# Two products in one vector instruction: the scan's steps and the power tables of a gated attention and state-space kernel

## The chip, the cores and the metric

The kernel runs on one core of a Trainium2 chip. The metric is the device time of one execution in microseconds; the median of three runs is given. The engines are called PE (TensorE, matrix products), ACT (ScalarE, here almost only exponentials), DVE (VectorE), POOL (GpSimd) and SP (the engine that issues most transfers).

## What is computed

Two branches over the same 2048 positions of 512 channels, mixed by a gate per position. Cut to what matters:

```python
g = sigmoid((x * gate_w).sum(-1, keepdims=True))
# a: attention with 32 heads of 16
p = softmax(q @ k.T * 16 ** -0.5)            # per head, 2048 x 2048
a = (p @ v, heads joined) @ wo
# b: a state-space layer, 512 channels with 128 complex states
logdA = exp(log_dt) * (A_re + 1j * A_im)
K[d, l] = real(sum_n C[d, n] * exp(logdA[d, n] * l) * exp(log_dt) * B[d, n])
b = causal_convolution(x, K) + x * Dskip
out = g * a + (1 - g) * b
```

## The kernel before

**Attention.** The 32 heads times 2048 queries times 2048 keys are cut into 2048 tiles of 128 keys by 512 queries. Four tiles (four heads at the same keys) are a *quad*, 64 tiles a *block*; there are 32 blocks. Tiles are taken in 683 groups of three: PE writes the scores of a group into one of two PSUM tiles `SC` (`qk`), ACT takes the exponential of the whole group in one activation (`ex`, line 907) into the ring `ET`, and PE multiplies by the values (`pv`) into `OA`. Transposes and normalizing of a finished block (`norm_a`, `norm_b`, `norm_c`) are on DVE.

**Exponentials on DVE.** Some tiles are done by DVE instead. A *set* is one quad of keys whose four tiles are taken out of four consecutive groups, one from each (`SHAPE`), so that the activation has two tiles in place of three. DVE turns the scores into the bits of an approximate power of two (`bits`, line 943, into `DZ`), and two further instructions per set (`batch`, line 954) make two shifted copies (`DU`, then `DZ` again); PE sums the three with values scaled for them (`VS`, made in `vscaled`, line 929). Sets are only allowed in windows of the group number (`WIN`: from group, to group, how many sets may be in flight, how many classes of key tiles), for which buffers have to fit into SBUF.

**State-space branch.** The convolution is done in chunks of 64 positions. `params` computes powers of the complex factor per channel and state on DVE: `L1`, `L2`, ... `L48`, and `MU`, the factor of a whole chunk; the copies `D16`, `D32`, `D48` (line 1145) hold each value twice side by side, as bf16. `base` makes the first 16 powers (`B16`), and `table` the other 48 from them: for each of eight pairs of channel blocks, for each m in 1 to 3 and for the real and the imaginary part, two products of 1024 columns into `tt1` and `tt2`, and their difference or sum into `PT` (all recorded by the helper `tt`, line 1001). That is 48 parts. `kstage` makes the convolution's kernel within a chunk from the tables, `sstage` the sums that each chunk hands on (evicted at line 1304 into `SG`; 16 blocks, marks `S0` to `S15`), and `scan` runs over the chunks. It has two halves of 256 channels (`scan0`, `scan1`), each 30 steps on DVE:

| line | what a step does, 512 columns of fp32 each |
|---|---|
| 1331 | `s2` = G (real, imaginary) times the real part of MU |
| 1333 | `s3` = G (imaginary, real) times the imaginary part of MU, negated for the first |
| 1336 | `s2` = `s2` + SG of this chunk |
| 1339 | `G` = `s2` + `s3` |
| 1342 | SG of this chunk = `G`, as bf16 |

The state `G` makes the steps a chain. `ystage` then turns the states into outputs (loads `yloads`, `xyloads`; products from `Py` and `Tt`; line 1415).

**What sets the order.** The program is written by a planner at build time. It keeps a clock per engine with a cost for every instruction, and picks at each point the piece of work (a generator's next step) that could start first; priorities break ties, and work that is not ready within 0.02 us is ranked as if it started 0.3 us from now at the earliest. The groups of attention are the backbone: after each activation, `fill` adds other work until the clock of ACT has been reached; work on PE may run `OVER` past it. `FILL` is a floor of PE work, counted in columns over the last `HWIN` = 3 us; what is missing is filled with products of zeros (`zero`). `DLAG` is the delay the planner assumes from a DVE result to PE, `DMARG` the one after a transfer, `PTM` that after the store of a table. A new set is begun in `decide` when a window and a buffer are open and DVE has collected enough idle time in the planner's clock:

```python
            plan["used"] = max(plan["used"], idle() - DVCAP)
            if plan["set"] is None and clear(x) and idle() - plan["used"] >= dvq():
                plan["used"] += dvq()
```

`dvq()` takes the first entry of `DVQ` whose mark has been passed. So the number of sets, and with it the work of ACT, follows from the idle time that the planner sees on DVE.

Dependences on the same engine count as well: a DVE instruction that reads what an earlier one wrote waits on DVE's own semaphore for it.

Of the kernel before, what the change touches and what calls it, by code (L numbers as in the profile page):

```python
# [13 lines left out]
P = 128  # L14
# [8 lines left out]
HALF_PI = math.pi / 2  # L23
NDSEM = 56
ZCOL = .216 / 512
FILL = 3500
EVERY = 2
XAT = "base0"
HWIN = 3.0
OVER = .6  # L30
DLAG = 0.6
TURN = dict(F=.105, R=.105, C=.105, H=.06)
DMARG = 2.4
PTM = 5.0
ZLAG = .6
BARE = 1
NS = 15
# [8 lines left out]
LEFT = 4  # L46
VSW = 152
VSP = [len(k) * VSW for k in VKT]  # L48
VSAT = (158, 500)
WIN = ((170, 475, 2, 1), (475, 540, 3, 1), (540, 678, 4, 2))  # L50
DVQ = (("scan1", 0.0), ("scan0", 0.5), ("S15", 1.0), (None, 0.5))
BP = 2.2
DVCAP = 2.0
BUP = 1
VW = 136
VG = 4 * VW + 16

# [355 lines left out]
def declare(nc, es):  # L413
    B = {}

    def sb(name, free, dt=BF16):
        B[name] = Buf(name, "sb", free, dt)


    sb("KT", 4 * S)  # L420
    sb("Q", 512)
    sb("Qs", 4 * 512)
    sb("Qm", 2 * 512)
    sb("VE", 16 * VG)
# [48 lines left out]
    for n in ("L1", "L2", "L4", "L8", "L16", "L32", "L48"):  # L473
        sb(n, 2 * D, FP32)
    sb("MU", 3 * D, FP32)
    sb("pt1", 2 * D, FP32)
    sb("pt2", 2 * D, FP32)
    for n in (16, 32, 48):
        for k in range(4):
            sb(f"D{n}.{k}", 4 * P)  # L480

    sb("FP", 2 * 128 * 8, FP32)
    sb("ft1", 2 * 64 * 8, FP32)
    sb("ft2", 2 * 64 * 8, FP32)
    for k in range(4):
        sb(f"B16{k}", 2 * 128 * 16)

    sb("PT", 2 * 2 * CB * T)
    sb("tt1", 2 * CB * 16)
    sb("tt2", 2 * CB * 16)  # L490
    sb("Qt", 2 * 32 * 128)
    sb("Kst", 2 * 8 * P)

    sb("SG0", 33 * 2 * SGH)
    sb("SG1", 33 * 2 * SGH)
    sb("G", 2 * 256, FP32)
    for n in ("s2", "s3"):
        sb(n, 2 * 256, FP32)
# [111 lines left out]
def record(nc, p, B, ins):  # L610
# [458 lines left out]
    def params():  # L1069
# [69 lines left out]
        for o, x, y in (("L16", "L8", "L8"), ("L32", "L16", "L16"), ("L48", "L16", "L32"), ("MU", "L32", "L32")):  # L1139
            yield from cmul("DVE", o, x, y)  # L1140
            if o != "MU":
                for k in range(4):
                    yield ("DVE", .35)
                    d, l = B[f"D{o[1:]}.{k}"], B[o]
                    op("DVE", lambda v, d=d, l=l, k=k: v.tensor_copy(d(0, [[2 * P, 2], [2, P], [1, 2]]), l(P * k, [[D, 2], [1, P], [0, 2]])),
                       [(l, 0)], [(d, 0)], c=.34)
# [15 lines left out]
        sch.mark("wb")  # L1162
        MU = B["MU"]
        yield ("DVE", 0.4)
        op("DVE", lambda v: v.tensor_scalar(MU(2 * D, [[1, D]]), MU(D, [[1, D]]), -1.0, None, ALU.mult), key("MU"), [(MU, 1)], c=.4)
        sch.mark("scanpar")

    def base(qr, eng):
# [36 lines left out]

    def table():
        yield ("AFTER", "D48")
        t1, t2 = B["tt1"], B["tt2"]
        H10 = dv(1024, 2)
        for pb in range(NBLK // 2):  # L1210
            qr, blks = pb // 2, (2 * pb, 2 * pb + 1)
            yield ("AFTER", f"base{qr}")
# [11 lines left out]
            for m in range(1, 4):  # L1224
                Dm = B[f"D{16 * m}.{qr}"]
                for part in range(2):
                    for ti, xr, yr in ((t1, 0, part), (t2, 1, 1 - part)):
                        yield ("DVE", H10)
                        tt("DVE", lambda ti=ti: ti(0, [[16, 2 * CB], [2, 8], [1, 2]]),
                           lambda xr=xr, b0=b0, B16=B16: B16(xr * 2048 + b0, [[16, 2 * CB], [2, 8], [1, 2]]),  # L1230
                           lambda yr=yr, d0=d0, Dm=Dm: Dm(yr * 2 * P + 2 * (d0 % P), [[2, 2 * CB], [0, 8], [1, 2]]), ALU.mult,
                           bk + [(Dm, 0)], [(ti, 0)], H10)
                    yield ("DVE", H10)
                    tt("DVE", lambda part=part, m=m: PT(part * CB * T + 16 * m, [[PTN, 2], [T, CB], [1, 16]]),
                       lambda: t1(0, [[CB * 16, 2], [16, CB], [1, 16]]), lambda: t2(0, [[CB * 16, 2], [16, CB], [1, 16]]),
                       ALU.add if part else ALU.subtract, [(t1, 0), (t2, 0)], W, H10)
# [73 lines left out]


    def scan():
        G, s2, s3 = B["G"], B["s2"], B["s3"]
        MU = B["MU"]
        e = "DVE"

# [2 lines left out]
        def pair(h):  # L1319
# [4 lines left out]
            for c in range(NCH - 1):  # L1324
                so = 2 * SGH * (c + 1)
                if c == 0:
                    yield (e, .34)
                    op(e, lambda v, so=so: v.tensor_copy(G(0, W), sg(so, [[SGH, 2], [1, 256]])), ks, [(G, 0)], c=.34)
                    continue
                yield (e, F5)  # L1330
                op(e, lambda v: v.tensor_tensor(s2(0, W), G(0, W), MU(d0, [[0, 2], [1, 256]]), ALU.mult), key("G", "MU"), [(s2, 0)], c=F5)  # L1331
                yield (e, F5)
                op(e, lambda v: v.tensor_tensor(s3(0, W), G(256, [[-256, 2], [1, 256]]), MU(D + d0, [[D, 2], [1, 256]]), ALU.mult),  # L1333
                   key("G", "MU") + [(MU, 1)], [(s3, 0)], c=F5)
                yield (e, F5)
                op(e, lambda v, so=so: v.tensor_tensor(s2(0, W), s2(0, W), sg(so, [[SGH, 2], [1, 256]]), ALU.add),  # L1336
                   [(s2, 0)] + ks, [(s2, 0)], c=F5)
                yield (e, F5)
                op(e, lambda v: v.tensor_tensor(G(0, [[1, 512]]), s2(0, [[1, 512]]), s3(0, [[1, 512]]), ALU.add),  # L1339
                   [(s2, 0), (s3, 0)], [(G, 0)], c=F5)  # L1340
# [29 lines left out]
        sch.mark(f"yl{u}")  # L1370

    def yloads():
        yield ("AFTER", "S12")
        for u in range(2 * NBLK):
            if u >= 3:
                yield ("AFTER", f"yu{u - 3}")
# [95 lines left out]

    def xyloads():
        for qr in range(4):
            yield ("AFTER", f"yu{8 * qr - 5}" if qr else "S12")
            yield from xload(B[f"XY{qr}"], qr)
            sch.mark(f"xy{qr}")

# [333 lines left out]
```

## Time and profile before

| | |
|---|---|
| median of three runs | 839.67 us (838.98 to 843.0) |
| the profiled execution | 841.1 us, span 839.3 us |
| ACT busy | 818.9 us, 98% of the span |
| DVE busy | 788.4 us, 94% |
| PE busy | 696.9 us, 83% |
| mean granted clock of PE | 0.983 of full speed |
| tiles on DVE (instructions of line 943) | 256, that is 64 sets |

Busy times of an engine are the union of its instructions, and neighbours on one engine overlap at their ends, so that the mean duration of a group is longer than what an instruction adds. A row of groups gives line, engine, operation, tiles, shapes and count, then busy time, mean duration in ns, and the idle time ahead of them with its releaser. A row of stretches gives the busy time and the number of instructions of each engine, then the granted clock, the share of the transfer engines and GB/s.

### The profile page before, as it was taken

The numbers are of one execution on the slowest core, as the hardware profiler recorded it, in microseconds if no ns is written. First come the engines' busy times: TensorE is split into PE (matmuls) and PEld (weight loads), VectorE is DVE, ScalarE is ACT, GpSimd is POOL, SyncE is SP. The second block draws the span as 40 slices with busy tenths as digits, with TensorE's granted clock in tenths as the row PEclk, the third lists the DMA queues.
The fourth block names the chain that finished last, engine by engine and source line by source line (L and its number), as shares of the span: only waits on it lengthen the run. The fifth ranks groups of instructions, "written<-read, shape, count | busy, mean of one in ns | idle before, by whom it ended". The sixth has DMA issues, their size and how long they took to land.

```text
span 839.3 us, 21027 instructions
## 1 busy us (share of the span) xinstructions
PE 696.9 (83%) x8977; PEld 253.4 (30%) x9002; DVE 788.4 (94%) x1344; ACT 818.9 (98%) x695; POOL 11.0 (1%) x13
## 2 busy tenths in 40 slices
PE   7787777778778888887787888789887889999987
PEld 3232332222212333332232332244432223444322
DVE  5799999998899999999999999999999989999996
ACT  7999999999999999999999999999999999999986
POOL 4000000000000000000000000000000000000000
PEclk9999999998999999999999999999999999999989
DMA  9650044792450789983392692066664025555113
GB/s 206 148 78 11 23 76 98 198 228 56 135 174 5 213 108 219 138 207 65 137 149 38 97 176 46 1 146 164 168 147 125 4 74 112 124 131 135 28 40 98
DMA packets 247954, 94.91 MB, mean 113 GB/s; under 512 B 222644, under 2 KB 234804, under 8 KB 245812
## 3 DMA queue, kind: packets, MB, share of 16 engines
q1 hardware_dynamic: 245988, 92.51, 50.1%
q10 hardware_dynamic: 1872, 1.05, 0.6%
q8 instruction: 71, 1.16, 0.5%
q14 instruction: 23, 0.19, 0.1%
HBM read 33.08 MB, written 35.01 MB: 81 GB/s over the span
## 4 chain that ended last, share of the span: by engine, by line
ACT 91%; PE 5%; DVE 2%; DMA 1%; issue 0%; ACTq 0%; DVEq 0%
ACT ET L907 91%; PE SC L626 2%; PE OA L626 2%; DMA Wk<-in_A_wqkv_dram 1%; DVE DZ L943 1%; PE MB L626 0%; DVE DZ L954 0%; DVE AR L1565 0%; DVE OT L978 0%; ACTq L630 0%; DVE Kst L1272 0%; DVE ON L990 0%; DVE OnT L997 0%; DVE KT L716 0%; DVE fo L1776 0%
## 5 line engine op out<-in xcount | busy, mean ns | idle before, releaser
L907 ACT ACTIVATE ET<-SC 128x1536 bf16<-128x1536 f32 (+1 forms) x683 | 810.6, 1545 | 8.4 <-PE SC L626 6.6
L626 PE MATMUL SC<-Qm,KT 32*128 32x512 bf16 x2048 | 279.1, 389 | 124.0 <-ACT ET L907 107.4
L626 PE MATMUL OA<-wm 128*32 128x512 bf16 (+3 forms) x1390 | 205.8, 369 | 1.2 <-DVE wm L679 1.2
L626 PE MATMUL OA<-ET,VE 128*32 128x512 bf16 x1792 | 180.8, 396 | 2.0 <-DVE OT L978 1.0
L943 DVE TENSOR_SCALAR DZ<-SC 128x512 uint16<-128x512 f32 x256 | 170.1, 683 | 9.5 <-PE SC L626 7.9
L626 PEld LDWEIGHTS SC<-Qm,KT 32*128 32x128 bf16 x2048 | 71.2, 91 | 341.5 <-ACT ET L907 300.6
L626 PEld LDWEIGHTS OA<-ET,VE 128*32 128x32 bf16 x1792 | 45.7, 93 | 104.0 <-issue 98.1
L626 PEld LDWEIGHTS OA<-wm 128*32 128x32 bf16 (+2 forms) x1390 | 55.3, 96 | 26.4 <-issue 17.7
L954 DVE TENSOR_SCALAR DZ<-DZ 128x2048 uint16<-128x2048 uint16 x64 | 44.0, 688 | 4.2 <-PE OA L626 4.1
L1304 DVE TENSOR_SCALAR SG<-MB 128x512 bf16<-128x512 f32 x64 | 43.6, 682 | 0.6 <-PE MB L626 0.2
L954 DVE TENSOR_SCALAR DU<-DZ 128x2048 uint16<-128x2048 uint16 x64 | 43.4, 686 | 0.1
L626 PE MATMUL MB<-X,Qt 128*128 128x64 bf16 x512 | 43.0, 244 | 0.0
L1339 DVE TENSOR_TENSOR G<-s,s 128x512 f32<-128x512 f32 x60 | 41.2, 687 | 1.0
L1331 DVE TENSOR_TENSOR s<-G,MU 128x512 f32<-128x512 f32 x60 | 41.1, 685 | 0.0
L1333 DVE TENSOR_TENSOR s<-G,MU 128x512 f32<-128x512 f32 x60 | 41.0, 683 | 0.0
L1336 DVE TENSOR_TENSOR s<-s,SG 128x512 f32<-128x512 f32 x60 | 40.9, 682 | 0.0
L626 PEld LDWEIGHTS MB<-X,Qt 128*128 128x128 bf16 x512 | 28.8, 116 | 20.3 <-issue 20.3
L1001 DVE TENSOR_TENSOR ft<-FP,L 128x1024 f32<-128x1024 f32 (+1 forms) x32 | 34.5, 1084 | 0.2
L1001 DVE TENSOR_TENSOR PT<-tt,tt 128x1024 bf16<-128x1024 bf16 x48 | 32.8, 683 | 0.5
L626 PEld LDWEIGHTS MB<-Py,SG 128*32 128x32 bf16 x1024 | 27.9, 167 | 6.4 <-issue 3.7
L626 PE MATMUL MB<-Py,SG 128*32 128x64 bf16 x1024 | 28.8, 231 | 0.0
L1342 DVE CAST SG<-G 128x512 bf16<-128x512 f32 x60 | 25.4, 423 | 1.2
(167 smaller groups left out, 607.7 us busy)
## 6 DMA issues: line engine op xcount, KB each, us to landing
gm_ptd<-PT SPq DMA_DIRECT2D x16, 1024.0 KB, 5.9
Py<-gm_ptd SPq DMA_DIRECT2D x32, 512.0 KB, 4.6
gm_kpd<-Kst SPq DMA_DIRECT2D x16, 256.0 KB, 3.8
Tt<-gm_kpd SPq DMA_DIRECT2D x128, 32.0 KB, 3.3
gm_xrd<-in_A_x_dram SPq DMA_DIRECT2D x1, 2048.0 KB, 13.4
gm_xcd<-wm SPq DMA_DIRECT2D x4, 512.0 KB, 10.3
gm_xcd<-XR SPq DMA_DIRECT2D x32, 64.0 KB, 1.9
Wo<-in_A_wo_dram SPq DMA_DIRECT2D x4, 512.0 KB, 4.2
```

Of the source, the lines that this page charges most:

```text
L626: op("PE", lambda t: t.matmul(out(), lhsT(), rhs(), start=start, stop=stop, skip_group_check=True, **kw), R, W, c=c, lat=.15, a=a, cfg=cfg)
L907: op("ACT", lambda a: a.activation(ET(512 * e, [[1, 512 * n]]), sc(0, [[1, 512 * n]]), AF.Exp, scale=DH ** -0.5), [(sc, i, g) for i in ran ...
L943: op("DVE", lambda v: v.tensor_scalar(z.u16(512 * k, [[1, 512 * n]]), sc(512 * na, [[1, 512 * n]]), XS, XB, ALU.mult, ALU.add), [(sc, na + ...
L954: op("DVE", lambda v: v.tensor_scalar(t.u16(0, [[1, 2048]]), z.u16(0, [[1, 2048]]), float(STEP[k][0]), None, ALU.add), R, W, c=.07 + 2048 ...
L1001: op(eng, lambda v: v.tensor_tensor(o(), a(), b_(), f), R, W, c=c)
L1304: op("DVE", lambda v, kh=kh, part=part: v.tensor_scalar(sg(2 * SGH + SGH * part + CB * k8 + 16 * kh, [[2 * SGH, 32], [1, 16]]), MB(0, [[16 ...
L1331: op(e, lambda v: v.tensor_tensor(s2(0, W), G(0, W), MU(d0, [[0, 2], [1, 256]]), ALU.mult), key("G", "MU"), [(s2, 0)], c=F5)
L1333: op(e, lambda v: v.tensor_tensor(s3(0, W), G(256, [[-256, 2], [1, 256]]), MU(D + d0, [[D, 2], [1, 256]]), ALU.mult), key("G", "MU") + [(M ...
L1336: op(e, lambda v, so=so: v.tensor_tensor(s2(0, W), s2(0, W), sg(so, [[SGH, 2], [1, 256]]), ALU.add), [(s2, 0)] + ks, [(s2, 0)], c=F5)
L1339: op(e, lambda v: v.tensor_tensor(G(0, [[1, 512]]), s2(0, [[1, 512]]), s3(0, [[1, 512]]), ALU.add), [(s2, 0), (s3, 0)], [(G, 0)], c=F5)
L1342: op(e, lambda v, so=so: v.tensor_copy(sg(so, [[SGH, 2], [1, 256]]), G(0, W)), key("G"), ks if c < NCH - 2 else [(sg, k, (h, 'G')) for k i ...
```

## The change

1. The scan's two products become one of 1024 columns. `s2` grows to four pieces of 256 columns and takes in `s3`: G's real part times (real, imaginary) of MU, then G's imaginary part times (real, minus imaginary). For that MU has a fourth row, so that both pairs lie side by side: a copy of the real part at 2 D, the negated imaginary part at 3 D.
2. In the tables the two products of a part become one of 2048 columns into `tt1`, which takes in `tt2`. For that the copies D16, D32, D48 are laid out by halves of 64 channels with real and imaginary parts side by side; each copy of 512 columns is done as two of 256.
3. Settings: FILL, OVER, DLAG, DMARG, PTM, BUP, the first entry of DVQ; the first window opens at group 180 in place of 170, and the scaled values for it are made at group 168 in place of 158; `yloads` and the first `xyloads` begin after S15 in place of S12.

```diff
-FILL = 3500
+FILL = 3600
...
-OVER = .6
-DLAG = 0.6
+OVER = 0.8
+DLAG = 0.7
...
-DMARG = 2.4
-PTM = 5.0
+DMARG = 2.6
+PTM = 4.0
...
-VSAT = (158, 500)
-WIN = ((170, 475, 2, 1), (475, 540, 3, 1), (540, 678, 4, 2))
-DVQ = (("scan1", 0.0), ("scan0", 0.5), ("S15", 1.0), (None, 0.5))
+VSAT = (168, 500)
+WIN = ((180, 475, 2, 1), (475, 540, 3, 1), (540, 678, 4, 2))
+DVQ = (("scan1", 0.3), ("scan0", 0.5), ("S15", 1.0), (None, 0.5))
...
-BUP = 1
+BUP = 2
...
-    sb("MU", 3 * D, FP32)
+    sb("MU", 4 * D, FP32)
...
                 for k in range(4):
-                    yield ("DVE", .35)
-                    d, l = B[f"D{o[1:]}.{k}"], B[o]
-                    op("DVE", lambda v, d=d, l=l, k=k: v.tensor_copy(d(0, [[2 * P, 2], [2, P], [1, 2]]), l(P * k, [[D, 2], [1, P], [0, 2]])),
-                       [(l, 0)], [(d, 0)], c=.34)
+                    for h in range(2):
+                        yield ("DVE", .22)
+                        d, l = B[f"D{o[1:]}.{k}"], B[o]
+                        op("DVE", lambda v, d=d, l=l, k=k, h=h: v.tensor_copy(d(2 * P * h, [[P, 2], [2, P // 2], [1, 2]]), l(P * k + 64 * h, [[D, 2], [1, P // 2], [0, 2]])),
+                           [(l, 0)], [(d, h)], c=.21)
...
-        op("DVE", lambda v: v.tensor_scalar(MU(2 * D, [[1, D]]), MU(D, [[1, D]]), -1.0, None, ALU.mult), key("MU"), [(MU, 1)], c=.4)
+        op("DVE", lambda v: v.tensor_scalar(MU(3 * D, [[1, D]]), MU(D, [[1, D]]), -1.0, None, ALU.mult), key("MU"), [(MU, 1)], c=.4)
+        op("DVE", lambda v: v.tensor_copy(MU(2 * D, [[1, D]]), MU(0, [[1, D]])), key("MU"), [(MU, 1)], c=.4)
...
-                    for ti, xr, yr in ((t1, 0, part), (t2, 1, 1 - part)):
-                        yield ("DVE", H10)
-                        tt("DVE", lambda ti=ti: ti(0, [[16, 2 * CB], [2, 8], [1, 2]]),
-                           lambda xr=xr, b0=b0, B16=B16: B16(xr * 2048 + b0, [[16, 2 * CB], [2, 8], [1, 2]]),
-                           lambda yr=yr, d0=d0, Dm=Dm: Dm(yr * 2 * P + 2 * (d0 % P), [[2, 2 * CB], [0, 8], [1, 2]]), ALU.mult,
-                           bk + [(Dm, 0)], [(ti, 0)], H10)
+                    yield ("DVE", H20)
+                    tt("DVE", lambda: t1(0, [[16, 4 * CB], [2, 8], [1, 2]]), lambda part=part, b0=b0, B16=B16: B16(b0 + 2048 * part, [[2048 - 4096 * part, 2], [1, 1024]]),
+                       lambda pb=pb, Dm=Dm: Dm(8 * CB * (pb % 2), [[2, 4 * CB], [0, 8], [1, 2]]), ALU.mult,
+                       bk + [(Dm, pb % 2)], [(t1, 0)], H20)
...
-                op(e, lambda v: v.tensor_tensor(s2(0, W), G(0, W), MU(d0, [[0, 2], [1, 256]]), ALU.mult), key("G", "MU"), [(s2, 0)], c=F5)
-                yield (e, F5)
-                op(e, lambda v: v.tensor_tensor(s3(0, W), G(256, [[-256, 2], [1, 256]]), MU(D + d0, [[D, 2], [1, 256]]), ALU.mult),
-                   key("G", "MU") + [(MU, 1)], [(s3, 0)], c=F5)
+                yield (e, F10)
+                op(e, lambda v: v.tensor_tensor(s2(0, [[512, 2], [256, 2], [1, 256]]), G(0, [[256, 2], [0, 2], [1, 256]]),
+                                                MU(d0, [[2 * D, 2], [D, 2], [1, 256]]), ALU.mult), key("G", "MU") + [(MU, 1)], [(s2, 0)], c=F10)
...
-                op(e, lambda v: v.tensor_tensor(G(0, [[1, 512]]), s2(0, [[1, 512]]), s3(0, [[1, 512]]), ALU.add),
-                   [(s2, 0), (s3, 0)], [(G, 0)], c=F5)
+                op(e, lambda v: v.tensor_tensor(G(0, W), s2(0, W), s2(768, [[-256, 2], [1, 256]]), ALU.add),
+                   [(s2, 0)], [(G, 0)], c=F5)
...
-        yield ("AFTER", "S12")
+        yield ("AFTER", "S15")
...
-            yield ("AFTER", f"yu{8 * qr - 5}" if qr else "S12")
+            yield ("AFTER", f"yu{8 * qr - 5}" if qr else "S15")
```

More of the change, by code (lines that the diff above doesn't have):

```diff
@@ L488, in declare @@
     sb("PT", 2 * 2 * CB * T)
-    sb("tt1", 2 * CB * 16)
-    sb("tt2", 2 * CB * 16)
+    sb("tt1", 4 * CB * 16)
     sb("Qt", 2 * 32 * 128)
@@ L496, in declare @@
     sb("G", 2 * 256, FP32)
-    for n in ("s2", "s3"):
-        sb(n, 2 * 256, FP32)
+    sb("s2", 4 * 256, FP32)
     for k in range(4):
@@ L1207, in table @@
         yield ("AFTER", "D48")
-        t1, t2 = B["tt1"], B["tt2"]
-        H10 = dv(1024, 2)
+        t1, H10, H20 = B["tt1"], dv(1024, 2), dv(2048, 2)
         for pb in range(NBLK // 2):
@@ L1226, in table @@
                 for part in range(2):
-                    for ti, xr, yr in ((t1, 0, part), (t2, 1, 1 - part)):
-                        yield ("DVE", H10)
-                        tt("DVE", lambda ti=ti: ti(0, [[16, 2 * CB], [2, 8], [1, 2]]),
-                           lambda xr=xr, b0=b0, B16=B16: B16(xr * 2048 + b0, [[16, 2 * CB], [2, 8], [1, 2]]),
-                           lambda yr=yr, d0=d0, Dm=Dm: Dm(yr * 2 * P + 2 * (d0 % P), [[2, 2 * CB], [0, 8], [1, 2]]), ALU.mult,
-                           bk + [(Dm, 0)], [(ti, 0)], H10)
+                    yield ("DVE", H20)
+                    tt("DVE", lambda: t1(0, [[16, 4 * CB], [2, 8], [1, 2]]), lambda part=part, b0=b0, B16=B16: B16(b0 + 2048 * part, [[2048 - 4096 * part, 2], [1, 1024]]),
+                       lambda pb=pb, Dm=Dm: Dm(8 * CB * (pb % 2), [[2, 4 * CB], [0, 8], [1, 2]]), ALU.mult,
+                       bk + [(Dm, pb % 2)], [(t1, 0)], H20)
                     yield ("DVE", H10)
                     tt("DVE", lambda part=part, m=m: PT(part * CB * T + 16 * m, [[PTN, 2], [T, CB], [1, 16]]),
-                       lambda: t1(0, [[CB * 16, 2], [16, CB], [1, 16]]), lambda: t2(0, [[CB * 16, 2], [16, CB], [1, 16]]),
-                       ALU.add if part else ALU.subtract, [(t1, 0), (t2, 0)], W, H10)
+                       lambda: t1(0, [[CB * 16, 2], [16, CB], [1, 16]]), lambda: t1(1024, [[CB * 16, 2], [16, CB], [1, 16]]),
+                       ALU.add if part else ALU.subtract, [(t1, 0)], W, H10)
             for i, blk in enumerate(blks):
@@ L1312, in scan @@
     def scan():
-        G, s2, s3 = B["G"], B["s2"], B["s3"]
+        G, s2 = B["G"], B["s2"]
         MU = B["MU"]
@@ L1329, in pair @@
                     continue
-                yield (e, F5)
-                op(e, lambda v: v.tensor_tensor(s2(0, W), G(0, W), MU(d0, [[0, 2], [1, 256]]), ALU.mult), key("G", "MU"), [(s2, 0)], c=F5)
-                yield (e, F5)
-                op(e, lambda v: v.tensor_tensor(s3(0, W), G(256, [[-256, 2], [1, 256]]), MU(D + d0, [[D, 2], [1, 256]]), ALU.mult),
-                   key("G", "MU") + [(MU, 1)], [(s3, 0)], c=F5)
+                yield (e, F10)
+                op(e, lambda v: v.tensor_tensor(s2(0, [[512, 2], [256, 2], [1, 256]]), G(0, [[256, 2], [0, 2], [1, 256]]),
+                                                MU(d0, [[2 * D, 2], [D, 2], [1, 256]]), ALU.mult), key("G", "MU") + [(MU, 1)], [(s2, 0)], c=F10)
                 yield (e, F5)
```

## The prediction

> **What bounds the kernel now.** I read the page first: busy times, slices, the chain.
>
> ```profile
> span 839.3 us, 21027 instructions
> PE 696.9 (83%) x8977; PEld 253.4 (30%) x9002; DVE 788.4 (94%) x1344; ACT 818.9 (98%) x695; POOL 11.0 (1%) x13
> ...
> ACT 91%; PE 5%; DVE 2%; DMA 1%; issue 0%; ACTq 0%; DVEq 0%
> ```
>
> ScalarE (ACT) is busy for 98% of the span and is 91% of the chain, nearly all of it the exponentials of line 907. VectorE (DVE) is at 94%. So time can come off in two ways only: ACT is given less to do, or its 20 us of idle time shrink. DVE can take exponentials from ACT: a set of four tiles costs DVE four instructions of L943 and two of L954. What a tile is worth to ACT follows from three pieces of the chain, and from the number of L943 instructions beside the second and the third.
>
> ```profile
> 15.22 171.90 ACT ET L907 x128
> 254.22 422.96 ACT ET L907 x354
> 680.76 46.27 ACT ET L907 x47
> ...
> 254.22:677.18 422.96, 83.55 (x124) 1.00 0.57 118
> 680.76:727.03 46.27, 25.90 (x40) 1.00 0.42 97
> ```
>
> With three tiles an activation takes 171.90 / 128 = 1.343 us. In the third piece 40 of the 47 have two tiles: (46.27 - 7 x 1.343) / 40 = 0.922 us; the second piece gives (422.96 - 230 x 1.343) / 124 = 0.920. A tile moved to DVE saves ACT 0.42 us, a set of four 1.69 us.
>
> Then the busy time by stages (columns: stretch; PE, PEld, DVE, ACT, POOL busy; clock, DMA share, GB/s; the last row counts L943 alone):
>
> ```profile
> 40.00:240.00 200.00, 156.44 (x1617) 51.26 (x1624) 189.62 (x306) 198.48 (x150) 0.00 (x0) 0.97 0.45 100
> 240.00:254.00 14.00, 10.79 (x101) 2.63 (x97) 13.24 (x24) 11.86 (x12) 0.52 (x1) 0.89 0.49 192
> 254.00:390.00 136.00, 116.53 (x1379) 42.43 (x1383) 130.36 (x221) 135.78 (x120) 0.00 (x0) 1.00 0.71 143
> 390.00:540.00 150.00, 121.31 (x1464) 43.19 (x1466) 147.73 (x255) 150.00 (x122) 0.53 (x1) 1.00 0.51 94
> 540.00:690.00 150.00, 125.67 (x2128) 49.96 (x2123) 145.86 (x262) 149.70 (x125) 0.00 (x0) 0.99 0.46 113
> 690.00:820.00 130.00, 121.79 (x1926) 47.52 (x1922) 124.00 (x207) 126.06 (x131) 0.00 (x0) 0.97 0.42 99
> ...
> 240.00:254.00 14.00, 5.17 (x8) 0.89 0.49 192
> ```
>
> From 40 to 820 us DVE idles 10.4 + 0.8 + 5.6 + 2.3 + 4.1 + 6.0 = 29.2 us, ACT 1.5 + 2.1 + 0.2 + 0.3 + 3.9 = 8.0 us. DVE is the scarce helper, and a microsecond freed on it buys exponentials. ACT's waits lie before 254 us, partly under a granted clock of 0.89, and after 690 us, where PE is 94% busy.
>
> **What one instruction costs DVE.** The mean of a group is not the cost, since neighbours overlap; the timeline gives starts (start, duration).
>
> ```profile
> L1331 DVE TENSOR_TENSOR s<-G,MU 128x512 f32<-128x512 f32 x60 | 41.1, 685 | 0.0
> L1001 DVE TENSOR_TENSOR ft<-FP,L 128x1024 f32<-128x1024 f32 x24 | 29.1, 1218 | 0.2
> ...
> 91.48 2.35 DVE L1001 TENSOR_TENSOR pt<-L,L 128x1024 f32<-128x1024 f32 x2
> ...
> 404.28 0.68 DVE L1333 TENSOR_TENSOR s<-G,MU 128x512 f32<-128x512 f32 x1
> 404.88 0.69 DVE L1336 TENSOR_TENSOR s<-s,SG 128x512 f32<-128x512 f32 x1
> 405.60 0.69 DVE L1339 TENSOR_TENSOR G<-s,s 128x512 f32<-128x512 f32 x1
> ...
> 685.58 0.69 DVE L1333 TENSOR_TENSOR s<-G,MU 128x512 f32<-128x512 f32 x1
> 686.18 0.69 DVE L1336 TENSOR_TENSOR s<-s,SG 128x512 f32<-128x512 f32 x1
> ```
>
> By the means the fusion looks rich: 2 x 0.685 - 1.218 = 0.15 us a step. By the starts it is poor: 0.60 us from L1333 to L1336, and 2.35 - 1.22 = 1.13 us between the two products of 1024. Two of 512 against one of 1024: 1.20 - 1.13 = 0.07 us. And L1339, which needs what L1336 wrote, starts 0.72 us after it: a result that is needed at once costs 0.12 us more than one that is not.
>
> **The scan.** Sixty steps save 60 x 0.07 = 4.2 us of DVE. But L1336 reads the product of L1331, and today L1333 stands between them and covers the wait. With one product there is no cover unless other work happens to stand there. In this trace L1336 starts right behind L1333 in 34 of the 60 steps (the first and the last are the pairs above). I take that share for the new wait: 34 x 0.12 = 4.1 us. Net gain 0.1 us; bounds +4.2 (always covered) and 60 x (0.07 - 0.12) = -3.0 (never). The Trainium skill says the opposite on waits (VectorE: DVE Perf Modes, "The DRAIN you can't avoid"): a semaphore after each DVE instruction costs nothing extra. By that rule the scan would be worth the whole 4.2 us, and the total 1.3 us less than below; the starts above, 0.72 against 0.60 us, speak against it.
>
> **The tables.** Forty-eight sums (PT from tt), each behind two products of 1024, which become one of 2048.
>
> ```profile
> L1001 DVE TENSOR_TENSOR PT<-tt,tt 128x1024 bf16<-128x1024 bf16 x48 | 32.8, 683 | 0.5
> ...
> 255.73 1.29 DVE L1001 TENSOR_TENSOR tt<-B,D16.2_151 128x1024 bf16<-128x1024 bf16 x2
> 257.06 0.69 DVE L1001 TENSOR_TENSOR PT<-tt,tt 128x1024 bf16<-128x1024 bf16 x1
> ...
> L1565 DVE TENSOR_TENSOR AR<-AR,Yl 128x2048 bf16<-128x2048 bf16 x3 | 6.8, 2281 | 0.0
> ```
>
> A product lasts 0.69 and the pair 1.29, so the second starts 0.60 after the first: the same as 512 columns of fp32, two columns in the time of one. The sum waits already (1.33 = 0.60 + 0.73), and will. If 2048 keep that rate they cost 1.13 as 1024 fp32 columns do: 48 x 0.07 = +3.4 us. No 2048-column product of this shape runs today; the other end is L1565 at 2.28 us, which reads one operand with stride two. I take 1.13, since the new operands keep runs of at least two neighbours as the old ones do; 2.28 is a rival.
>
> **Copies.** Twelve copies (L1145) become 24 of half the size, and one copy of 512 is added for MU.
>
> ```profile
> 97.02 0.42 DVE L1145 CAST D48.0_157<-L 128x512 bf16<-128x512 f32 x1
> 97.36 0.42 DVE L1145 CAST D48.1_158<-L 128x512 bf16<-128x512 f32 x1
> ```
>
> One costs 0.34, of which 0.07 stays when it is halved: 24 x 0.205 - 12 x 0.34 = 0.84 us, and 0.34 for MU. Together -1.2 us of DVE, between 80 and 115 us, where only later table work waits for it.
>
> **From DVE to time.** DVE gains 0.1 + 3.4 - 1.2 = 2.3 us (bounds -0.8 and +6.4).
>
> ```profile
> L943 DVE TENSOR_SCALAR DZ<-SC 128x512 uint16<-128x512 f32 x256 | 170.1, 683 | 9.5 <-PE SC L626 7.9
> L954 DVE TENSOR_SCALAR DZ<-DZ 128x2048 uint16<-128x2048 uint16 x64 | 44.0, 688 | 4.2 <-PE OA L626 4.1
> ```
>
> These last as long as L1331, so I price them at 0.60 too: a set is 6 x 0.60 = 3.6 us of DVE. It shortens the run by 1.69 us, in which DVE can do nothing either, so 5.3 us of DVE buy one set: 0.32 us of time per us of DVE. The term is -0.7 us (+0.3 to -2.0). If the planner makes no more sets of it, it is nothing.
>
> **The settings**, of which the trace shows no other value; each is bounded by what it can touch. The first window opens 10 groups later: 8 tiles lie in 240 to 254 us, so up to 8 x 0.42 = 3.4 us; DVE was 95% busy there with tables queued behind, so most comes back later. I take a quarter, +0.9. The threshold of 0.3 us idle per set after the second scan: 29 sets in 690 to 820 (131 activations, 115 of them shared by the L943 count of that stretch) would ask for 8.6 us where 6.0 are idle; 2.6 / 3.9 = 0.7 set, 1.1 us at most, I take +0.5.
>
> ```profile
> 690.00:820.00 130.00, 75.19 (x115) 0.97 0.42 99
> ```
>
> FILL (3% more filler work on PE), OVER, DLAG and DMARG decide how far PE runs ahead and how late the planner thinks data is: they can remove ACT's 7.5 us of waits before 254 and after 690, leave them, or double them. I take half back, -3.8, because the waits before 254 us go with the lowered clock, which filler work holds up. Of DVE's 29.2 idle us I take a fifth as usable, 5.8 x 0.32 = -1.9. These two are the weak terms. Loads for the Y stage that begin at S15, not S12, cost nothing, for the last eviction of an S stage (L1304) lies before 520 us and the first product from Py at 544:
>
> ```profile
> 500.00:520.00 20.00, 4.11 (x6) 1.00 0.44 75
> 520.00:540.00 20.00, 0.00 (x0) 1.00 0.02 5
> ...
> L626 PE MATMUL MB<-Py,SG x1024: 192/238/264, 543.9 to 795.3; 128*32 128x64 bf16 x171
> ```
>
> BUP 2 only reorders work of DVE; if another block's sums then wait for it, that is part of the doubling above.
>
> Sum: -0.7 + 0.9 + 0.5 - 3.8 - 1.9 = -5.0 us. The profiled execution took 841.1 us (span 839.3 and 1.8 around it), the median is 1.4 lower: 836.1 for a like execution, **834.7** for the median.
>
> **Rivals.** (a) The settings move no wait: then only -0.7 + 0.9 + 0.5 = +0.7 us remain, 840.4. For it: the fused instructions themselves buy almost nothing. Against: there are 7.5 us of ACT waits to win. (b) PE becomes the bound after 690 us. It is 94% busy there; with a higher FILL and a larger OVER more filler stands ahead of the scores that ACT waits for. It decides once PE passes ACT in that stretch, 4 us of extra PE work; from there each of 131 activations is late. At 0.08 us each it is +10.5, less the 5.0 of above: 845. Against: in 540 to 690, PE at 84%, ACT waits 0.3 us. (c) The 2048-column product falls to the rate of L1565: 48 x (2.28 - 1.20) = 52 us of DVE, x 0.32 = +16.6, less the settings: about 853. Against it the page Vector Engine (DVE) Microarchitecture Reference of the Trainium skill (5.1) asks only for 16-bit operands with an innermost step of one, which holds here; it says that a negative step, which one of the two products has in its outer dimension, was not measured. No run here shows it. (d) The scan's new wait is always covered: the 4.1 us return, -1.3 more, 833.4; the 34 pairs without cover speak against it. The rule on semaphores above would have it so.
>
> **Chances.** Half a per cent, 4.2 us, is what a measurement of this kernel can tell from no change. The forecast, below 835.5: 0.46, of which (d) 0.08. Rival (a) and smaller gains: 0.34. Slower 0.20: (b) 0.12, (c) 0.03, the late window not made up for 0.05. The range takes in the forecast with all the waits recovered and the scan's waits covered (834.7 - 3.8 - 1.3 = 829.6, so 829) and rival (b) at its price (845); (c) and the worse half of (b) lie outside, and gains beyond the bounds.
>
> **What would show it.** The fused scan product: 60 instructions near 1.22 us with the next start 1.13 to 1.25 later, and L1336 behind it at 1.25 where nothing stands between. Tables: 48 products near 1.22; 2.28 means (c). L943 count: 256 and a few (each four more are 1.69 us of ACT); fewer than 256 means that the window or threshold cost more than the fusion gave. ACT idle before 254 and after 690 below 7.5 us if the settings did their part, above it for (b). I am wrong if the count falls and ACT's waits stay.

## The result, and the profile after

The changed kernel takes 848.71 us (median of four runs, 847.8 to 851.11), the kernel before 840.76 beside it: a ratio of 1.0095, 95% interval 1.0074 to 1.0116. It is slower by 8 us where 834.7 was forecast. The profiled execution took 847.8 us. From its page, the same lines as of before:

```profile
span 845.9 us, 21476 instructions
PE 715.6 (85%) x9262; PEld 259.8 (31%) x9262; DVE 786.7 (93%) x1255; ACT 817.8 (97%) x695; POOL 11.0 (1%) x13
...
ACT 79%; DVE 10%; PE 6%; DMA 3%; issue 1%; SPq 1%; ACTq 0%; DVEq 0%
```

ScalarE's work is 1.1 us less (817.8 after 818.9), yet the span is 6.6 us longer: its idle time rose from 20.4 to 28.1 us. Its share of the chain fell from 91% to 79%, and DVE (2% before) holds 10%. The busy time by stages tells where:

```profile
40.00:240.00 200.00, 155.91 (x1675) 51.22 (x1672) 187.57 (x290) 193.18 (x145) 0.00 (x0) 0.97 0.44 100
240.00:254.00 14.00, 10.27 (x133) 2.85 (x125) 9.27 (x22) 14.00 (x12) 0.52 (x1) 1.00 0.49 193
254.00:390.00 136.00, 118.15 (x1377) 41.36 (x1377) 128.88 (x198) 132.68 (x117) 0.52 (x1) 0.99 0.67 147
390.00:540.00 150.00, 130.86 (x1544) 47.10 (x1544) 146.24 (x227) 149.22 (x127) 0.00 (x0) 0.99 0.50 89
540.00:690.00 150.00, 130.06 (x2099) 51.79 (x2099) 146.98 (x235) 149.56 (x126) 0.00 (x0) 1.00 0.49 115
690.00:820.00 130.00, 120.46 (x2002) 48.37 (x2002) 123.28 (x210) 129.38 (x132) 0.00 (x0) 1.00 0.38 89
820.00:845.90 25.90, 18.72 (x177) 5.26 (x173) 18.98 (x25) 15.05 (x15) 0.00 (x0) 0.93 0.34 108
```

The last stretch of the kernel before, for comparison:

```profile
820.00:839.30 19.30, 13.27 (x131) 4.22 (x129) 11.99 (x21) 12.10 (x12) 0.00 (x0) 0.97 0.24 83
```

ACT's idle time between 40 and 240 us rose from 1.5 to 6.8 us, between 254 and 390 from 0.2 to 3.3, and after 820 from 7.2 to 10.9. It fell from 2.1 to nothing between 240 and 254, and from 3.9 to 0.6 between 690 and 820. The rise before 240 and the one after 820 are the two losses that the experiments follow.

**The first loss, read backwards.** The timelines of DVE, PE and ACT of the changed kernel, in order of time (start, duration, what was done, in brackets the idle time before and what ended it):

```profile
157.91 0.43 DVE L1221 COPY PT<-B 128x1024 bf16<-128x1024 bf16 x1 [3.43 <-DMA gm_ptd<-PT]
160.92 0.43 DVE L1221 COPY PT<-B 128x1024 bf16<-128x1024 bf16 x1 [2.58 <-DMA gm_ptd<-PT]
...
163.60 0.71 DVE L976 STREAM_TRANSPOSE OT<-OA 128x512 f32<-128x512 f32 x1
...
164.36 0.62 PE L624 MATMUL OA<-ET,VE 128*32 128x512 bf16 x4 [5.84 <-DVE OT L976]
...
166.86 1.45 ACT L905 ACTIVATE ET<-SC 128x1536 bf16<-128x1536 f32 x1 [6.32 <-PE SC L624]
```

From the last line up: ACT waits 6.3 us for scores. PE is held by the transpose of a finished block (L976); that stands in DVE's queue behind two copies (L1221) into `PT`, which wait for the stores of the table before. In the kernel before the same copies ran without a wait, the transpose ahead of them:

```profile
157.05 0.72 DVE L978 STREAM_TRANSPOSE OT<-OA 128x512 f32<-128x512 f32 x1
...
158.27 0.74 DVE L1222 COPY PT<-B 128x1024 bf16<-128x1024 bf16 x2
```

SP's queue shows why the stores are late. First the kernel before, then the changed one, then a row of the changed one's waits of SP (us in total, times, longest; L261 is a helper's line) and one of its DVE:

```profile
99.28 0.34 SPq L1597 DMA_DIRECT2D gm_qd<-Qs  x1
99.66 3.46 SPq L1455 DMA_TRANSPOSE XR<-gm_xrd  x2
...
146.85 0.92 SPq L1239 DMA_DIRECT2D gm_ptd<-PT  x2
```

```profile
101.12 0.34 SPq L1592 DMA_DIRECT2D gm_qd<-Qs  x1
115.88 2.54 SPq L1450 DMA_TRANSPOSE XR<-gm_xrd  x2
...
153.84 0.88 SPq L1236 DMA_DIRECT2D gm_ptd<-PT  x2
```

```profile
SPq L261 <- DVE nwi L999: 14.4, 1, 14.4
```

```profile
115.12 0.68 DVE L999 TENSOR_TENSOR nwi<-u,u 128x512 bf16<-128x512 f32 x1
```

SP stood for 14.4 us at the first load of the turned input (`XR`), until DVE had made `nwi` at 115.8, a result that has nothing to do with XR. The stores of `PT` behind it on SP start at 153.84, though the last sum of that table is already being made at 143.74. The tie between `nwi` and XR is memory. The planner orders the work first and gives out the addresses afterwards (`place`, which lets buffers whose spans of groups don't meet share bytes). The new order was given an XR that lies over four older buffers, DVE's temporary `u4` among them, and `nwi` is the last to read `u4`. So the load waits for bytes, and the planner, done by then, had not counted that.

**The second loss.** DVE's and ACT's timelines at the end:

```profile
827.10 2.28 DVE L1560 TENSOR_TENSOR AR<-AR,Yl 128x2048 bf16<-128x2048 bf16 x1
829.30 0.68 DVE L941 TENSOR_SCALAR DZ<-SC 128x512 uint16<-128x512 f32 x1
829.90 4.48 DVE L1560 TENSOR_TENSOR AR<-AR,Yl 128x2048 bf16<-128x2048 bf16 x2
834.30 0.69 DVE L952 TENSOR_SCALAR DZ<-DZ 128x2048 uint16<-128x2048 uint16 x1
...
838.08 0.72 DVE L976 STREAM_TRANSPOSE OT<-OA 128x512 f32<-128x512 f32 x1 [1.59 <-PE OA L624]
...
840.79 0.58 ACT L1769 CAST fo<-MB 128x512 bf16<-128x512 f32 x1 [6.11 <-PE MB L624]
```

The state-space branch's last gated output `Yst` comes at 816.7 us (797.0 before), so the three additions of 2048 columns run at 827 to 834, ahead of the last set's shifted copies (L952), and ACT, done with its last exponential at 834.7, waits 6.1 us for the projection of the output. Before, they ran at 806.9 to 819.9, and the wait was half as long:

```profile
834.17 0.58 ACT L1774 CAST fo<-MB 128x512 bf16<-128x512 f32 x1 [3.25 <-PE MB L626]
```

All sixteen programs of this case divide in the same way. In six (the changed kernel and a_store_first, ts, s_only, a_place, c_prio of the experiments below) the last addition ends within 3 us of ACT's last exponential, and the wait is 5.7 to 7.7 us. In the other ten it ends 10 us or more ahead of it, and the wait is 3.1 to 3.4 us.

### The profile page after: what moved, and what is told of

Same layout as the page of the kernel before. It is cut to its first block, busy times and chain, and to the rows that moved or that the text cites. A ratio compares the mean times of both kernels' runs of the same rounds, so it can differ in the third digit from the quotient of the medians.

```text
span 845.9 us, 21476 instructions
## 1 busy us (share of the span) xinstructions
PE 715.6 (85%) x9262; PEld 259.8 (31%) x9262; DVE 786.7 (93%) x1255; ACT 817.8 (97%) x695; POOL 11.0 (1%) x13
## 4 chain that ended last, share of the span: by engine, by line
ACT 79%; DVE 10%; PE 6%; DMA 3%; issue 1%; SPq 1%; ACTq 0%; DVEq 0%
ACT ET L905 79%; PE SC L624 3%; PE OA L624 2%; DMA gm_ptd<-PT 2%; PE MB L624 1%; DVE tt L999 1%; DVE ft L999 1%; DVE DZ L941 1%; DMA Wk<-in_A_wqkv_dram 1%; DVE AR L1560 1%; DVE s L1328 1%; DVE PT L999 1%; DVE SG L1301 1%; DMA Tt<-gm_kpd 0%; DVE OT L976 0%
## 5 line engine op out<-in xcount | busy, mean ns | idle before, releaser
L624 PE MATMUL SC<-Qm,KT 32*128 32x512 bf16 x2048 | 282.0, 387 | 103.2 <-ACT ET L905 86.8
L624 PE MATMUL OA<-wm 128*32 128x512 bf16 (+3 forms) x1634 | 218.9, 356 | 1.2 <-DVE wm L677 1.2
L624 PE MATMUL OA<-ET,VE 128*32 128x512 bf16 x1788 | 178.8, 394 | 7.2 <-DVE OT L976 5.8
L624 PEld LDWEIGHTS SC<-Qm,KT 32*128 32x128 bf16 x2048 | 73.1, 91 | 321.0 <-ACT ET L905 272.2
L1328 DVE TENSOR_TENSOR s<-G,MU 128x1024 f32<-128x1024 f32 x60 | 73.1, 1218 | 0.0
L624 PEld LDWEIGHTS OA<-wm 128*32 128x32 bf16 (+2 forms) x1634 | 61.0, 96 | 30.8 <-issue 18.9
L952 DVE TENSOR_SCALAR DZ<-DZ 128x2048 uint16<-128x2048 uint16 x65 | 44.6, 686 | 3.3 <-PE OA L624 3.0
L952 DVE TENSOR_SCALAR DU<-DZ 128x2048 uint16<-128x2048 uint16 x65 | 44.2, 684 | 0.2
L1334 DVE TENSOR_TENSOR G<-s 128x512 f32<-128x512 f32 x60 | 41.1, 685 | 1.0
L999 DVE TENSOR_TENSOR PT<-tt 128x1024 bf16<-128x1024 bf16 x48 | 32.6, 679 | 0.1
L976 DVE STREAM_TRANSPOSE OT<-OA 128x512 f32<-128x512 f32 x32 | 22.7, 710 | 5.9 <-PE OA L624 5.6
L624 PE MATMUL OA<-DZ,VS 128*32 128x512 bf16 x260 | 25.6, 384 | 0.8 <-DVE DZ L952 0.8
```

What stands on the lines that cost most here:

```text
L624: op("PE", lambda t: t.matmul(out(), lhsT(), rhs(), start=start, stop=stop, skip_group_check=True, **kw), R, W, c=c, lat=.15, a=a, cfg=cfg)
L952: op("DVE", lambda v: v.tensor_scalar(t.u16(0, [[1, 2048]]), z.u16(0, [[1, 2048]]), float(STEP[k][0]), None, ALU.add), R, W, c=.07 + 2048 ...
L976: op("DVE", lambda v: v.transpose(OT(512 * w, [[1, 512]]), OA(0, [[1, 512]])), [(OA, 0, b)], [(OT, w, b)], c=.64)
L999: op(eng, lambda v: v.tensor_tensor(o(), a(), b_(), f), R, W, c=c)
L1328: op(e, lambda v: v.tensor_tensor(s2(0, [[512, 2], [256, 2], [1, 256]]), G(0, [[256, 2], [0, 2], [1, 256]]), MU(d0, [[2 * D, 2], [D, 2], [ ...
L1334: op(e, lambda v: v.tensor_tensor(G(0, W), s2(0, W), s2(768, [[-256, 2], [1, 256]]), ALU.add), [(s2, 0)], [(G, 0)], c=F5)
```

## The experiments

Each was timed in five rounds beside the kernel before (840.66 to 841.6 us); ratios are to that.

**Which part of the change.** One part at a time on the kernel before. The settings alone (set_only):

> The kernel before with all settings of the change and none of the joined products. If the settings are what costs (theory 3: margins and the later window): 845 to 849, with waits of ACT before 254 us or after 690 us above the 7.5 us of the kernel before. If they cost nothing by themselves: 839 to 842.

843.73 us, 1.0031 [1.0016, 1.0046], between the two ranges. Still 64 sets (256 instructions of L943). The waits of ACT before 254 and after 690 us fell from 7.5 to 5.2 us (up to 820), but 3.7 us stand between 254 and 390, where the kernel before has 0.2. The two products, with the old settings, together (ts) and each alone (t_only, s_only; where the scan is joined, MU has three rows, so that no row is copied):

```diff
-MU(d0, [[2 * D, 2], [D, 2], [1, 256]])
+MU(D + d0, [[-D, 2], [D, 2], [1, 256]])
```

> Both joined products with the settings of before; so that it fits beside the early window, MU keeps three rows (minus imaginary, real, imaginary) and the second pair is read one row lower, which also saves the copy of MU. By the prediction's sum for DVE (2.3 us and 0.34 for the copy) the gain is 0.8 us of time if waits stay as they are: 839 to 841. If the joined products themselves cost (a longer instruction ahead of short urgent ones): above 843. If they are worth more than I priced, sets go from 64 to 66 or more: below 838.

> Only the tables' products joined, with the settings of before. By the sum for DVE (48 x 0.07 gained, 0.84 for the split copies) 2.6 us of DVE or 0.8 us of time: 839 to 841.5, L943 instructions 256 to 264. If the long instruction costs by itself: above 843.

> Only the scan's products joined, with the settings of before and MU in three rows (minus imaginary, real, imaginary), so that nothing has to be copied. By the prediction the gain is 4.2 us of DVE less 4.1 us of new waits, so nothing: 840 to 842, with the instruction after the product starting 1.25 us after it where nothing stands between. If the new wait is always covered: 1.3 us less.

Both: 852.31, 1.0128 [1.0104, 1.0151], with 66 sets. Tables alone: 843.99, 1.0046 [1.0029, 1.0063]. Scan alone: 847.13, 1.0069 [1.0054, 1.0085], each with 65. No part is a gain; the three with joined products lie above their ranges, where two of the expectations put a cost of the joined products themselves (c_sset below speaks against that). And the parts do not add up: both joined products with the old settings lose more than with the new ones. That points to the order that each plan happens to get. In none of these four is the first load of XR held as in the changed kernel: it starts at 99.9 to 105.7 us. So the first loss comes and goes with single plans (a_ptm5 below has another like it), and other plans lose elsewhere: ts has 3.7 us of ACT's idle time between 390 and 540 and 6.3 between 540 and 690.

**Was it the order of the stores?** In the changed kernel's finished order, the first two stores of a table are issued ahead of the six transfers of the turned input that stand just before them on SP (a_store_first):

```diff
-        log = prog.log
+        log = store_first(prog.log)   # two gm_ptd stores ahead of six of XR and xcd
```

> The changed kernel with the same order on every engine but SP: the first two stores of a table are issued ahead of the six transfers of the turned input (XR, xcd) that stood just before them. Theory 1 (one stall: the store comes late, the two copies L1221 stand on DVE for 6.0 us and ACT starves for 6.3 us): the store is issued near 149 us in place of 153.8, the longest wait of ACT before 240 us falls from 6.3 to under 2 us, and 4 to 6 us of the 8 us come back: 842.5 to 844.5. Theory 2 (the late end of the state-space branch, its additions L1560 behind the last exponentials, sets the time whatever happens early): 847 to 849.

852.35, 1.0137 [1.0114, 1.016]: no gain, and above both ranges. The first stores did start at 146.90 in place of 153.84, but the waits show that the stall only moved to the next store (DVE's copy at 190.8, ACT at 197.3):

```profile
ACT ET L913 <- PE SC L632: 12.2, 10, 7.4
DVE PT L1229 <- DMA gm_ptd<-PT: 8.8, 2, 6.9
```

SP is late as a whole, and moving these two stores ahead does not cure that. One setting back (PTM, the margin after the store of a table) made a new plan (a_ptm5):

```diff
-PTM = 4.0
+PTM = 5.0
```

> The changed kernel with PTM at 5.0 as before, every other setting as changed; the whole program is planned anew. Theory 1: the planner puts the copies at least 1 us later behind the store, the wait of L1221 falls from 6.0 to under 3 us, 841 to 845. If the delay margin has nothing to do with it: 847 to 850.

855.61, 1.0176 [1.0158, 1.0193], the worst of all and above both ranges. Here XR lay over the weights of K, and its first load left at 117.16.

**Was it the place of XR?** The changed kernel, its order of work untouched; only the memory planner is told that XR is needed 16 groups earlier (a_place):

```diff
+        for n in ("XR",):
+            bufs[n].first -= 16
         place(nc, bufs)
```

> The changed kernel with every engine's instructions in the same order; only the bytes are given out differently: XR, the buffer of the turned input, is placed as if it were needed 16 groups earlier, so that it no longer lies on x0n, cb, u4 and pt1. In the changed kernel its first load stood on SP's queue for 14.7 us until DVE had last read u4 (nothing the planner knows of, since it gives out bytes after planning), and 36 transfers queued behind it, among them the first stores of a table. Theory 4 (the place of XR is the cause): the first load of XR is issued near 102 us in place of 115.9, the stores of the first two tables near 145 in place of 153.8, the wait of the copies L1221 (6.0 us) and the 6.3 us wait of ACT are gone, 842 to 844. Theory 2 (the late end of the state-space branch): 847 to 849.

843.2 us, 1.0024 [1.0005, 1.0043], from 848.71 (1.0095). The first XR load is back at 101.91, and the copies of PT have no wait:

```profile
101.91 2.55 SPq L1452 DMA_TRANSPOSE XR<-gm_xrd  x2
...
154.81 0.76 DVE L1223 COPY PT<-B 128x1024 bf16<-128x1024 bf16 x2
```

The edit is not a move of XR alone: `place` searches anew, and 115 of the 139 buffers get another address. So this run by itself shows that the layout costs 5.5 us, and the trace that the wait of XR is gone with it. (The profiled execution of this kernel took 848.86 us, far above its median, so its later stages are read with care.) The other direction, on the kernel before: only the wait is added, with everything else unchanged (b_wait).

```diff
+    log[i] = (f, q, (eng, fn, R + [(b["nwi"], 0)], W))   # i: the first load of XR
```

> The kernel before with one wait added after planning, all orders kept: the first load of XR also waits for the DVE instruction that last reads u4 (near 113 us). Theory 4: SP is 10 to 14 us late from there on, the table stores and the copies of the next tables with them, and ACT starves once or twice: 845 to 849. If SP has slack enough, as theory 1 would have it: 840 to 842.

849.79, 1.0106 [1.0088, 1.0124], just above the 845 to 849 expected: this one wait on a transfer queue, with every address as it was, costs as much as the whole change did. ACT's idle time between 40 and 240 us rises from 1.5 to 8.7. It goes the same way, through SP into DVE's queue and to ACT, only that PE waits here (3.9 us) for a projection's cast that stands behind the copies, not for a transpose:

```profile
113.73 2.54 SPq L1464 DMA_TRANSPOSE XR<-gm_xrd  x2
...
165.15 0.43 DVE L1231 COPY PT<-B 128x1024 bf16<-128x1024 bf16 x1 [2.36 <-DMA gm_ptd<-PT]
...
171.85 1.45 ACT L916 ACTIVATE ET<-SC 128x1536 bf16<-128x1536 f32 x1 [3.64 <-PE SC L635]
```

And the kernel with PTM at 5.0, with the same edit of XR's place (c_ptm5):

> The changed kernel with PTM back at 5.0 (which measured 855.61 us) and, as in the experiment before it with the buffer of the turned input, XR placed as if it were needed 16 groups earlier. Placement theory: the 16 us for which SP stood at the first XR load go, the copies of the tables' first parts no longer stand in DVE's queue, ScalarE's waits for score products fall from 18.7 to about 10 us, and the time falls by 7 to 9 us to 846.5 to 848.5. Rival (the 5.0 itself makes the order bad, the place of XR does not matter here): 853 to 857. With both the fused scan stays, so the additions at the end stay behind the last exponentials.

844.53, 1.0037 [1.0021, 1.0052]: 11 us less than without the edit, more than the 7 to 9 expected. The waits for score products fell from 18.7 to 6.9 us, further than the 10 expected; ACT's idle time between 40 and 240 us fell by 10.6 us (14.4 to 3.8), which is nearly all of the gain. The end had no part in it: ACT's wait there is 3.1 us in both.

**Was the rest the late end of the branch?** Two edits that bring it forward, both on the kernel with XR moved. The scan gets a higher priority (c_prio); or VectorE must show more idle time for each early set (c_early):

```diff
-scan(), 3
+scan(), 1
```

```diff
-DVQ = (("scan1", 0.3), ("scan0", 0.5), ("S15", 1.0), (None, 0.5))
+DVQ = (("scan1", 0.3), ("scan0", 0.5), ("S15", 1.0), (None, 0.8))
```

> The changed kernel with XR placed 16 groups earlier (843.2 us) and the scan's priority in the planner 1 in place of 3, so the recurrence goes ahead of the Y stage and the parameters when both are ready. Tail theory (with the joined product the state-space branch ends 12 to 20 us later, its three additions of 2048 columns fall behind the last exponentials, and ScalarE waits 6 to 7.6 us in place of 3.2 for the first projection of the output): the second half of the scan ends about 15 us earlier, the last Yst some 4 us earlier, the wait before the first output eviction falls to 3 to 5.5 us, the time to 840.5 to 842. Rival (what is left over the kernel before comes from the late loads of the Y stage, or from the product itself): 842.7 to 844.5.

> The changed kernel with XR placed 16 groups earlier (843.2 us) and the idle that VectorE must show before a set is taken, up to the end of the S products, 0.8 us in place of 0.5: fewer sets early, more room for the branch. Tail theory: the last Yst near 797 as in the kernel before, the three additions among the exponentials, the wait before the first output eviction 3.0 to 3.5 us; the time 840 to 842 with as many sets as before, and 1.1 us more for each set fewer. Rival (the tail costs nothing of its own): 843 to 845.

The first: 841.53, 1.0011 [0.9996, 1.0026], 65 sets, the wait still 5.7 us. The second: 841.15, 0.9994 [0.9979, 1.0009], 64 sets. ACT's end in the second:

```profile
817.61 13.79 ACT L907 ACTIVATE ET<-SC 128x1024 bf16<-128x1024 f32 x14 [0.23 <-PE OA L626]
834.75 0.58 ACT L1771 CAST fo<-MB 128x512 bf16<-128x512 f32 x1 [3.35 <-PE MB L626]
```

Its last Yst came at 788.6 and the additions at 799 to 810. Both times are those of the kernel before, within the interval. But both edits replan everything, so neither tests the tail alone. In the first the three additions still stand together, at 817.7 to 825.6, and the wait fell by little. In the second the idle time between 254 and 390 us went too (0.9 us, where the changed kernel has 3.3), and 3.1 us came between 390 and 540. So the late additions do lengthen the wait at the end, by about 3 us, as the sixteen programs show; that they are the 2 us left after a_place is argued, not shown. The joined scan with the new settings, tables apart (the Y loads begin at S12 as before, though the expectation says all settings; c_sset):

> The changed kernel with the tables' products apart again (two of 1024 columns a part, two buffers): the scan's joined product with all the new settings. XR then lies on no buffer that is read late. Tail theory: its branch is planned to end close to the kernel before, so the last Yst comes near 805, the wait before the first output eviction near 3.5 us, and the time is 841 to 843.5, under the 847.1 of the joined product with the old settings. Rival (the joined product costs time wherever it stands, by its waits for its own result): 845.5 to 848.

842.38, 1.0027 [1.0013, 1.0041], 5 us under the same product with the old settings. With the new settings the ratios are 1.0031 without a joined product, 1.0027 with that of the scan and 1.0024 with both (a_place): within the intervals, joining adds no cost of its own, and no gain.

**Does the extra set reach the time?** The edits of a_place and c_prio, and a smaller margin for transfers, whose plan ends the branch early (d_both); the second of the two also takes sets at the end without a threshold (d_both0):

```diff
-DMARG = 2.6
+DMARG = 2.4
```

> The changed kernel with XR placed 16 groups earlier and the scan at priority 1 (841.53 us), and DMARG, the time that the planner adds before it takes a transfer's data as there, back at 2.4: of these plans the one with 65 sets whose Y stage ends earliest. The last Yst should come near 790 to 795 us, the three additions before 815, the wait before the first output eviction 3.2 us in place of 5.7. If the joined products' one extra set reaches the time once both losses are gone: 838.5 to 840, faster than before by 0.1 to 0.3%. Rival (DVE's gain comes back as other waits whatever the order, or the smaller margin for transfers brings back waits): 840.5 to 843.

> As the run before it, with the threshold of idle for a set after the second half of the scan at 0.0 as in the kernel before, not 0.3: sets are taken as soon as VectorE idles at all. As many or more sets late. If a set is worth its 1.1 to 1.7 us of ScalarE: 838 to 840. Rival (late sets only fill VectorE where ScalarE then waits for it): 840.5 to 843.

844.68, 1.0036 [1.0022, 1.005], and 844.28, 1.0028 [1.001, 1.0045]. Both lie above both ranges. The first made 64 sets, not the 65 expected, the second 66; the wait at the end was 3.1 us in both, and by their medians they were slower than c_prio. Another loss stands in its place, in the Y stage. The first one's waits of PE and its row of that stage, then that stage's row of the scan alone with the old settings (also 2.4):

```profile
PE MB L626 <- DMA Tt<-gm_kpd: 2.1, 4, 1.0
PE MB L626 <- DMA Py<-gm_ptd: 2.0, 2, 1.7
```

```profile
540.00:690.00 150.00, 128.79 (x2122) 51.12 (x2119) 139.74 (x225) 144.50 (x121) 0.00 (x0) 0.97 0.48 114
```

```profile
540.00:690.00 150.00, 126.05 (x2004) 48.62 (x1999) 140.49 (x225) 144.40 (x121) 0.00 (x0) 0.95 0.47 113
```

ACT idles 5.5 and 5.6 us there, and PE waits 4.1 and 4.7 us for loads of the tables (Tt, Py), for which it does not wait there in the kernel before or in c_early. That these waits are the cause is a reading, not tested. In the kernels at 2.6 it is 0 to 1.8 us (c_early none; a_place, read with care, 3.6). All five versions with a joined product and 2.4 lose 3.7 to 6.3 us there; the kernel before, also at 2.4, loses 0.3. Why the loads come too late was not settled. Whether a set more than before can be kept without any of these losses stays open: no version here beat the kernel before.

## Why the prediction was wrong, step by step

**The prices were right.** The scan product costs what was said, and so do the tables. The row of the group; then, from the view of a tile, the four products of one power table (ns, min/median/max); then the timeline:

```profile
L1328 DVE TENSOR_TENSOR s<-G,MU 128x1024 f32<-128x1024 f32 x60 | 73.1, 1218 | 0.0
```

```profile
L999 DVE TENSOR_TENSOR tt<-B,D16.0_149 x4: 1181/1214/1219, 124.1 to 164.2; 128x2048 bf16<-128x2048 bf16 x4
```

```profile
140.87 1.21 DVE L999 TENSOR_TENSOR tt<-B,D48.0_157 128x2048 bf16<-128x2048 bf16 x1
142.00 1.21 DVE L999 TENSOR_TENSOR ft<-FP,L 128x1024 f32<-128x1024 f32 x1
```

A product of 2048 adds 1.13 us, the value taken; rival (c), 2.28 us, did not happen. In the scan, a step in which the sum follows the product at once, and one with other work between:

```profile
454.05 1.22 DVE L1328 TENSOR_TENSOR s<-G,MU 128x1024 f32<-128x1024 f32 x1
455.30 0.69 DVE L1331 TENSOR_TENSOR s<-s,SG 128x512 f32<-128x512 f32 x1
...
703.09 1.22 DVE L1328 TENSOR_TENSOR s<-G,MU 128x1024 f32<-128x1024 f32 x1
704.23 0.68 DVE L941 TENSOR_SCALAR DZ<-SC 128x512 uint16<-128x512 f32 x1
```

1.25 and 1.14: the wait of about 0.12 us was right, but it came in 20 of the 60 steps, not 34, so the scan gained 4.2 - 2.4 = 1.8 us of DVE where 0.1 was taken. Rival (d), always covered, fell too.

**From DVE to time** came out near: 65 sets, ACT's work 1.1 us shorter for a forecast of -0.7. But a set is the smallest step of this count, and plans with both joined products made 64 to 66, so the agreement is in part luck.

```profile
L941 DVE TENSOR_SCALAR DZ<-SC 128x512 uint16<-128x512 f32 x260 | 171.4, 682 | 7.5 <-PE SC L624 6.2
```

**The step that failed is the term of the settings**: -3.8 for half of ACT's waits recovered and -1.9 for a fifth of DVE's idle time put to use. Measured alone (set_only), the settings made the kernel 0.31% slower, about 2.6 us, where the prediction's four terms for them sum to -4.3. In the changed kernel ACT's waits after 690 us did go (3.9 to 0.6), but before 254 they rose from 3.6 to 6.8: together 7.4 for 7.5, where the doubling that the step allowed for and the halving that it took would both have been seen. The part about the clock came true in 240 to 254 us: the waits went (2.1 to 0) and the granted clock rose from 0.89 to 1.00. But t_only, with the old filler, shows the same there, so it is not shown that filler did it. And the step looked nowhere else: 3.1 us came from 254 to 390, 3.7 after 820. DVE's idle time from 40 to 820 us rose from 29.2 to 37.8.

The step bounded each setting by "what it can touch". But every setting, and every changed cost, makes a new order, and with it a new layout of memory. It never asked which buffer would come to lie over which, and what SP would then wait for; the sum has no term for that. It is the 5.5 us between this kernel and the one with the other layout (848.71 to 843.2), and the 9 us of the wait added to the kernel before. That XR was held in this plan, and in none of the plans of the parts, is an accident of the layout; that a new plan can bring such a wait is what the step left out.

The cause of the 3.1 us from 254 to 390 stays open. They come with the settings: set_only has 3.7 there as well, the versions with XR moved 3.5 to 5.3 but for 0.9 in c_early. They lie between 350 and 383 us, where PE waits 1.5 us, before it may write the next scores, for DVE to have read the last ones (into DZ), and the granted clock is 0.91 from 340 to 360 us (1.00 before).

**Rival (b)** gave the right sign and nearly the price (845) for the wrong reason: from 690 to 820 us ACT idled 0.6 us with PE at 93%, so PE did not become the bound. The sign named for being wrong, a falling count with the waits left, didn't show: the count rose, and the waits rose more. The tail, where the additions run into the last exponentials, is another term that the sum did not have.

## What to carry to other kernels

Where a planner writes the order and the memory, a change of one instruction is a change of the whole program: compare the queues for a transfer that moved far (14 us here) and ask whose bytes it waits for, before reading the changed instruction. An in-order queue passes such a wait on to all behind it: SP to the stores, DVE's copies to a transpose, PE, and at last the bounding engine. Test a suspected placement both ways: ask for another place in the slow kernel, its order kept, and add the wait alone to the fast one. The second is the cleaner test, since a new layout moves other buffers too.

## What the runs showed of the hardware

- Half of the 2048-column products read one operand with a negative outer step, half with a positive one. All 48 last 1.18 to 1.23 us, so the step's sign does not matter here. The Trainium skill (Vector Engine (DVE) Microarchitecture Reference, 5.1) leaves that unmeasured.
- A DVE instruction that needs the one just ahead of it starts 1.25 us after a product of 1024 fp32 columns (20 steps of the scan), and one that doesn't mostly 1.13 to 1.14 (34 of the other 40). The Trainium skill (VectorE: DVE Perf Modes, "The DRAIN you can't avoid") says of eight copies that a semaphore after each costs nothing extra. Here, where the next instruction needs the result, the wait costs 0.12 us.
- One more wait of 14 us on SP, off the chain of the bounding engine, cost 9 us of time (b_wait, 1.0106 [1.0088, 1.0124]).
